# A joint-attention block on one Trainium2 core: the first key block's scale as a TensorE column, a copy put into VectorE's wait for the norm, and transposes spread over the waits for scale rows

## The chip, the cores and the metric

The kernel runs on one NeuronCore of a Trainium2 chip. The metric is the device time of one execution in microseconds, as the median over several runs; lower is better. A core has TensorE (matmuls and transposes, results into PSUM), VectorE, ScalarE and GpSimd (elementwise work), SyncE (here: it issues the loads), and DMA engines that move data between HBM and the core's SBUF. The engines run side by side, each through its own queue in order, and wait for one another by semaphores.

## The reference

One image stream (batch B = 2, 256 tokens) and one text stream (2 x 32 tokens), width D = 1152, all bf16. A conditioning vector `c` gives shift, scale and gate per stream; both streams attend jointly.

```python
mod_i = (_silu(c) @ wmod_img).reshape(B, 6, 1, D)       # the same for text
shi, sci, gai = mod_i[:, 0], mod_i[:, 1], mod_i[:, 2]
hi = _layernorm(x_img) * (1 + sci) + shi                 # the same for text
qkvi = hi @ wqkv_img
q, k, v = text and image tokens of each, concatenated
p = _softmax(einsum('bqd,bkd->bqk', q, k) * D ** -0.5)
a = einsum('bqk,bkd->bqd', p, v)
out_i = x_img + gai * (ai @ wo_img)
out_t = x_txt + gat * (at @ wo_txt)
```

## The kernel before

The width is cut into KT = 9 blocks of 128, the image tokens into four tiles of 128 (tiles 0 and 1 are batch 0, tiles 2 and 3 batch 1). Matmuls contract over the width, so activations must stand transposed: width on the partitions, tokens along the free dimension. "Key block kt" below is one block of 128 of that contracted width.

The work starts with v of the image. The shift is left out of it at first and added later (`shift_v_rows`), so v needs only the normed tokens times the scale 1 + `sci`. What happens before the first v matmul is the part that the change touches:

- *Loads.* SyncE issues all of them in one order: the two batches of `x_img` (L104), the scale weights `w_sc_i` in four pieces (L108: rows 0 to 3, 4 to 6, 7, 8; a row is 128 x 1152, 288 KB), the v weights `w_v_i` in six pieces (L110: rows 0, 1, 2, 3 to 4, 5 to 6, 7 to 8), then the other 1152 x 1152 matrices, each into one of five slots when the slot comes free.
- *silu(c)* stands as columns `sT` (128 x 9 x 2) and, padded with zeros to 32 columns, as `sT32`.
- *Norm.* Tiles 0 and 2 get their sums on ScalarE (`ln_sums`), tiles 1 and 3 their statistics on VectorE (`ln_stats`); ScalarE makes 1/std (`ln_rstd`), VectorE applies it (`ln_norm`, L212), into `xn_i`.
- *Transposes.* `x_transposes(k0, b)` (L240) transposes three key blocks of one batch on TensorE into a PSUM tile `tp` (six transposes of 128 x 128) and returns the function that copies them out to `xT_i` (L250): VectorE for k0 = 3, ScalarE for k0 = 0 and 6.
- *Scale rows.* `sc_rows` (L230) makes the scale as rows: for each kt, four matmuls of 288 columns side by side, each in a column tile of 32 of the array, into `sc_ps`; the first four add the 1. `sc_cols` (L256) turns blocks of it by VectorE's 32 x 32 transpose, so that the scale stands as a column per key block in `sc1_i`.
- *Scaling.* `x_scale` (L260) multiplies `xT_i` by that column into `hS_i`, on VectorE.
- *v.* `v_open` (L271) runs matmuls of 512 columns over several (token tile, column chunk) pairs; `A0` are the four pairs of batch 0, `A1` two of batch 1. The first call takes kt = 0, 1, 2 for `A0`, the next the same for `A1`.
- *Warm-ups.* `warm_up(n)` (L132) runs n matmuls of ones into `wps`, whose result nobody uses.

`pin` keeps each engine's instructions in the order in which the program has them; lines 292 to 328 are that order, written out by hand. PSUM has two pools: `ps_mm` with six buffers and `ps_tr` with two, given out in turn.

After v the program runs shift and second scaling, q and k of image and text, the scores, softmax, the attention over v, and the two output projections with the gates. TensorE works through them in program order.

Of the kernel before, what the change touches and what calls it, by code (L numbers as in the profile page):

```python
# [14 lines left out]
def kernel(  # L15
# [14 lines left out]
    nc = tc.nc  # L30
    bf = mybir.dt.bfloat16
    f32 = mybir.dt.float32
    PSUM = bass.MemoryType.PSUM

    B, NI, D = x_img.shape
    NT = x_txt.shape[1]
    P = 128
    KT = D // P
    NTOK = NI + NT
    NIT = (B * NI) // P  # L40
    TPB = NI // P
# [13 lines left out]
    ps_mm = ctx.enter_context(tc.tile_pool(name="ps_mm", bufs=6, space=PSUM))  # L55
    ps_tr = ctx.enter_context(tc.tile_pool(name="ps_tr", bufs=2, space=PSUM))

    pin = tc.keep_in_program_order

    def mm(*a, **k):  # L60
        return pin(nc.tensor.matmul(*a, **k))  # L61

    def tr(*a, **k):
        return pin(nc.tensor.transpose(*a, **k))  # L64
# [11 lines left out]
    def wtile(slot):  # L76
        return wpool.tile([P, KT, D], bf, tag="w%d" % slot, name="t")
# [4 lines left out]
    K8 = KT - 1  # L82
# [17 lines left out]
    w_sc_i = wtile(0)  # L100
# [21 lines left out]
    warm = const.tile([P, 512], bf)  # L122
# [3 lines left out]
    unit = const.tile([P, LW], bf)  # L126
# [5 lines left out]
    def warm_up(n):  # L132
        for _ in range(n):
            mm(wps[:], lhsT=warm[:, 0:P], rhs=warm[:], start=True, stop=True)
# [33 lines left out]
    sT = const.tile([P, KT, B], bf)  # L168
# [16 lines left out]
    def ln_stats(x_ap, np_, between=None):  # L185
        stats = small.tile([P, NCH, 6], f32, tag="stats")
        for k in range(NCH):
            if k == 1 and between:
                between()
            pin(nc.vector.bn_stats(stats[0:np_, k, :], x_ap[:, k * CH:(k + 1) * CH]))  # L190
        mv = small.tile([P, 2], f32, tag="mv")
        pin(nc.vector.bn_aggr(mv[0:np_, :], stats[0:np_, :, :]))
        return mv

    def ln_sums(x_ap, junk):
        sm = small.tile([P, 3], f32, tag="lnact")
        pin(nc.scalar.activation(junk, x_ap, ACT.Copy, scale=1.0 / D, accum_out=sm[:, 0:1]))
        pin(nc.scalar.activation(junk, x_ap, ACT.Square, scale=float(D) ** -0.5, accum_out=sm[:, 1:2]))
        return sm

    def ln_var(sm):
        pin(nc.vector.scalar_tensor_tensor(sm[:, 2:3], sm[:, 0:1], sm[:, 0:1], sm[:, 1:2],
                                           op0=ALU.mult, op1=ALU.subtract))

    def ln_rstd(var, np_, sign=1.0):
        rstd = small.tile([P, 1], f32, tag="rstd")
        pin(nc.scalar.activation(rstd[0:np_, :], var, ACT.Ln, bias=eps_t[0:np_], scale=sign))
        pin(nc.scalar.activation(rstd[0:np_, :], rstd[0:np_, :], ACT.Exp, scale=-0.5))
        return rstd

    def ln_norm(x_ap, mean, rstd, np_, out_ap):
        pin(nc.vector.tensor_scalar(out_ap, x_ap, mean, rstd[0:np_, :], op0=ALU.subtract, op1=ALU.mult))  # L212

    xn_i = act.tile([P, NIT, D], bf, tag="A")
    hS_i = act.tile([P, KT, B * NI], bf, tag="Bt")
    xT_i = act.tile([P, KT, B * NI], bf)
# [3 lines left out]
    def group(w, kt, g):  # L220
        return w[:, kt, :].rearrange("p (c g l) -> p g c l", g=NGG, l=LW)[:, g]

    def mod_cols_of(gps, name):
        t = const.tile([P, KT, LW], f32, name=name, tag={"sctc": "shc"}.get(name, name))
        pin(nc.vector.transpose(t[:].rearrange("p c l -> p (c l)"), gps[:].rearrange("p c l -> p (c l)")))
        return t

    sc_ps = ps_mm.tile([P, KT, LW], f32, tag="mm")

    def sc_rows(r0, r1):  # L230
        if r0 == 0:
            for g in range(NGG):
                mm(sc_ps[LW * g:LW * g + LW].rearrange("p c l -> p (c l)"), lhsT=unit[:], rhs=warm[:, 0:KT * LW],
                   start=True, stop=False, tile_position=(0, LW * g))
        for kt in range(r0, r1):
            for g in range(NGG):
                mm(sc_ps[LW * g:LW * g + LW], lhsT=sT32[:, kt, :], rhs=group(w_sc_i, kt, g),
                   start=False, stop=(kt == KT - 1), tile_position=(0, LW * g))

    def x_transposes(k0, b):  # L240
        tr_pool = b == 1 or k0 < 6
        tp = (ps_tr if tr_pool else ps_mm).tile([P, 3, NI], bf, tag="tr" if tr_pool else "mm", name="tp")
        for kt in range(k0, k0 + 3):
            for t in range(TPB):
                i = b * TPB + t
                tr(tp[:, kt - k0, t * P:(t + 1) * P], xn_i[:, i, kt * P:(kt + 1) * P], ident[:])
        dst = xT_i[:, k0:k0 + 3, b * NI:(b + 1) * NI]

        def copy_out():
            pin(nc.vector.tensor_copy(dst, tp[:]) if k0 == 3 else nc.scalar.copy(dst, tp[:]))  # L250

        return copy_out

    sc1_i = const.tile([P, KT, LW], f32, name="scc", tag="scc")

    def sc_cols(c0, c1):  # L256
        pin(nc.vector.transpose(sc1_i[:, c0:c1, :].rearrange("p c l -> p (c l)"),
                                sc_ps[:, c0:c1, :].rearrange("p c l -> p (c l)")))

    def x_scale(k0, k1, b, step=TPB):  # L260
        for kt in range(k0, k1):
            for t in range(0, TPB, step):
                t0, t1 = b * NI + t * P, b * NI + (t + step) * P
                pin(nc.vector.tensor_scalar(hS_i[:, kt, t0:t1], xT_i[:, kt, t0:t1], sc1_i[:, kt, b:b + 1], None,  # L264
                                            op0=ALU.mult))

    VW = 512
# [3 lines left out]
    def v_open(ids, k0, k1, kt_major=True):  # L271
        for key in ids:
            if key not in accs:
                accs[key] = ps_mm.tile([P, VW], f32, tag="mm", name="vps")
        loop = [(kt, key) for kt in range(k0, k1) for key in ids] if kt_major else \
            [(kt, key) for key in ids for kt in range(k0, k1)]
        for kt, (i, cc) in loop:
            mm(accs[(i, cc)][:], lhsT=hS_i[:, kt, i * P:(i + 1) * P], rhs=w_v_i[:, kt, cc * VW:(cc + 1) * VW],
               start=(kt == 0), stop=(kt == KT - 1), skip_group_check=True)
            if kt == KT - 1:  # L280
                evac(v_i[:, i, cc * VW:(cc + 1) * VW], accs[(i, cc)][:])
# [4 lines left out]
    def ln_norm_dve(i, mv):  # L286
        ln_norm(x_i[:, i, :], mv[:, 0:1], ln_rstd(mv[:, 1:2], P), P, xn_i[:, i, :])

    def ln_norm_act(i, sm):
        ln_norm(x_i[:, i, :], sm[:, 0:1], ln_rstd(sm[:, 2:3], P, sign=-1.0), P, xn_i[:, i, :])  # L290
# [3 lines left out]
    ln_var(s0)  # L294
    ln_norm_dve(1, m1)
    ln_norm_act(0, s0)
    s2 = ln_sums(x_i[:, 2, :], xn_i[:, 2, :])
    m3 = ln_stats(x_i[:, 3, :], P)
    ln_var(s2)
    r3, r2 = ln_rstd(m3[:, 1:2], P), ln_rstd(s2[:, 2:3], P, sign=-1.0)  # L300
    ln_norm(x_i[:, 3, :], m3[:, 0:1], r3, P, xn_i[:, 3, :])
    ln_norm(x_i[:, 2, :], s2[:, 0:1], r2, P, xn_i[:, 2, :])
    for out in [x_transposes(k0, 0) for k0 in (0, 3, 6)]:
        out()
    sc_rows(0, 4)
    warm_up(3)
    sc_rows(4, 7)
    out01 = x_transposes(0, 1)
    out31 = x_transposes(3, 1)
    sc_rows(7, K8)  # L310
    sc_rows(K8, KT)
    out61 = x_transposes(6, 1)
    out01()
    sc_cols(0, 1)
    x_scale(0, 1, 0, step=1)
    sc_cols(1, 5)
    x_scale(1, 3, 0)
    v_open(A0, 0, 3)
    out31()
    out61()  # L320
    x_scale(0, 3, 1)
    sc_cols(5, KT)
    for k0 in (3, 6):
# [436 lines left out]
```

## Time and profile before

| | us |
|---|---|
| median of 9 runs | 118.66 |
| lowest, highest | 118.17, 119.2 |
| the profiled execution | 119.2 |
| its span in the profile | 117.1 |
| TensorE busy (matmuls) | 111.0 |
| VectorE, ScalarE, GpSimd busy | 72.3, 44.2, 12.4 |
| first v matmul starts | 15.16 |

The profile is of one execution. PE is TensorE's matmuls, PEld its weight loads, DVE VectorE, ACT ScalarE, POOL GpSimd, SPq SyncE's queue of DMA issues. A line of a timeline has start, length, engine, source line, operation, what it writes and reads, the shape and the count of merged instructions, and in brackets the idle time before it with what ended it. The source line of a matmul is that of the helper `mm` (L61), of a transpose that of `tr` (L64), so those are told apart by what they write: `sc_ps` the scale rows, `tp` the transposes, `vps` v, `wps` the warm-ups. `t` stands for any weight matrix. The chain of waits follows the work that ended last back to its start: at each step to what released it, or to the instruction before it on its engine. A matmul's length in the trace includes the time in which it drains, so the pace of a row of them is read from start to start.

### The profile page before, as it was taken

The numbers are of one execution on the slowest core, as the hardware profiler recorded it, in microseconds if no ns is written. First come the engines' busy times: TensorE is split into PE (matmuls) and PEld (weight loads), VectorE is DVE, ScalarE is ACT, GpSimd is POOL, SyncE is SP. The second block draws the span as 40 slices with busy tenths as digits, with TensorE's granted clock in tenths as the row PEclk, the third lists the DMA queues.
The fourth block names the chain that finished last, engine by engine and source line by source line (L and its number), as shares of the span: only waits on it lengthen the run. The fifth ranks groups of instructions, "written<-read, shape, count | busy, mean of one in ns | idle before, by whom it ended". The sixth has DMA issues, their size and how long they took to land.

```text
span 117.1 us, 2569 instructions
## 1 busy us (share of the span) xinstructions
PE 111.0 (95%) x1072; PEld 63.6 (54%) x1072; DVE 72.3 (62%) x153; ACT 44.2 (38%) x92; POOL 12.4 (11%) x34
## 2 busy tenths in 40 slices
PE   5998799999999999999999999999999999999990
PEld 1245444444594444445444448787866666566670
DVE  3578296043787999999997040017758608666571
ACT  4799520023473288924330324135647500100000
POOL 7300000000000000000000000002450700451000
PEclk9999999999999999999999999999999999999999
DMA  3999999999999999999999999999999999822223
GB/s 109 368 342 395 404 411 405 412 412 410 412 405 406 314 392 411 407 409 412 413 351 403 411 412 413 405 411 405 412 405 409 408 423 366 318 103 58 101 50 101
DMA packets 18917, 41.02 MB, mean 350 GB/s; under 512 B 1323, under 2 KB 1851, under 8 KB 18907
## 3 DMA queue, kind: packets, MB, share of 16 engines
q1 hardware_dynamic: 18032, 39.85, 88.9%
q0 software_dynamic: 480, 0.89, 2.2%
q10 hardware_dynamic: 395, 0.12, 0.4%
q8 instruction: 8, 0.13, 0.4%
q14 instruction: 2, 0.02, 0.0%
HBM read 39.52 MB, written 1.34 MB: 349 GB/s over the span
## 4 chain that ended last, share of the span: by engine, by line
PE 84%; DMA 9%; DVE 2%; SPq 1%; ACT 1%; issue 1%; DVEq 0%
PE ps L61 52%; PE vps L61 15%; DMA t<-in_wmod_img_dram 9%; PE gps L61 5%; PE aps L61 5%; PE sps L61 4%; DVE tmp L701 1%; PE sc_ps L61 1%; DVE o L702 1%; SPq L104 1%; PE tp L64 1%; ACT pT L621 1%; PE pT_ps L64 0%; SPq L108 0%; PE tpt L64 0%
## 5 line engine op out<-in xcount | busy, mean ns | idle before, releaser
L61 PE MATMUL ps<-xT_i,t 128*128 128x512 bf16 x162 | 35.7, 380 | 0.0
L61 PEld LDWEIGHTS <-t 128*128 128x128 bf16 x324 | 20.5, 98 | 19.0 <-issue 0.6
L435 DVE SCALAR_TENSOR_TENSOR acc_sh<-t,sTf,acc_sh 128x1152 f32<-128x1152 bf16 x16 | 21.4, 1404 | 0.0
L61 PE MATMUL ps<-t,aT 128*128 128x384 bf16 (+3 forms) x153 | 20.3, 308 | 0.0
L61 PE MATMUL vps<-t,hS_i 128*128 128x512 bf16 (+1 forms) x108 | 17.9, 326 | 0.1
L61 PEld LDWEIGHTS <-aT 128*128 128x128 bf16 (+1 forms) x153 | 13.0, 101 | 7.1 <-issue 0.8
L61 PEld LDWEIGHTS <-hS_i 128*128 128x128 bf16 x108 | 9.0, 98 | 8.8 <-DVE hS_i L264 0.4
L365 ACT CAST qkT<-ps 128x512 bf16<-128x512 f32 (+2 forms) x11 | 6.1, 551 | 15.0 <-PE ps L61 13.7
L701 DVE TENSOR_TENSOR tmp<-ps,gb 128x384 bf16<-128x384 f32 (+2 forms) x13 | 6.8, 524 | 7.9 <-PE ps L61 4.1
L587 POOL TENSOR_SCALAR pb<-e,rs 128x32 bf16<-128x32 f32 (+1 forms) x5 | 2.2, 445 | 77.1 <-DVE rs L584 77.1
L61 PE MATMUL wps<-warm 128*128 128x512 bf16 x25 | 8.1, 482 | 1.5 <-DVE unit L127 1.5
L363 ACT ACTIVATE qkT<-ps 128x512 bf16<-128x512 f32 (+2 forms) x11 | 6.1, 561 | 8.7 <-PE ps L61 7.0
L180 DVE CAST v_i<-vps 128x512 bf16<-128x512 f32 x5 | 3.5, 692 | 7.5 <-PE vps L61 7.5
L572 DVE TENSOR_REDUCE nmx<-sps 128x1 f32<-128x288 f32 x4 | 1.8, 458 | 9.6 <-PE sps L61 9.6
L61 PEld LDWEIGHTS <-sT 128*32 128x32 bf16 x180 | 4.7, 96 | 3.6 <-issue 3.0
L182 ACT CAST v_i<-vps 128x512 bf16<-128x512 f32 x4 | 2.3, 580 | 9.9 <-PE vps L61 9.9
L634 DVE TENSOR_SCALAR aT<-aps,svc 128x288 bf16<-128x288 f32 x9 | 4.3, 517 | 2.2 <-PE aps L61 2.2
L61 PEld LDWEIGHTS <-warm 128*128 128x128 bf16 x25 | 2.7, 117 | 5.2 <-issue 2.4
L61 PE MATMUL sps<-qkT 128*128 128x288 bf16 (+1 forms) x54 | 5.3, 287 | 0.0
L61 PE MATMUL ps<-hT_t,t 128*128 128x64 bf16 x162 | 5.2, 194 | 0.0
L61 PE MATMUL gps<-t,sT 128*32 128x288 bf16 x144 | 5.2, 287 | 0.0
L61 PE MATMUL aps<-pT,v_i 128*128 128x288 bf16 x36 | 5.1, 287 | 0.1
(111 smaller groups left out, 105.2 us busy)
## 6 DMA issues: line engine op xcount, KB each, us to landing
t<-in_wqkv_txt_dram SPq DMA_DIRECT2D x3, 2592.0 KB, 18.8
t<-in_wmod_img_dram SPq DMA_DIRECT2D x2, 2592.0 KB, 13.8
t<-in_wmod_txt_dram SPq DMA_DIRECT2D x2, 2592.0 KB, 17.9
t<-in_wqkv_img_dram SPq DMA_DIRECT2D x3, 864.0 KB, 13.7
t<-in_wqkv_img_dram SPq DMA_DIRECT2D x1, 2592.0 KB
t<-in_wo_img_dram SPq DMA_DIRECT2D x3, 864.0 KB, 9.5
t<-in_wqkv_img_dram SPq DMA_DIRECT2D x3, 576.0 KB, 10.4
t<-in_wmod_txt_dram SPq DMA_DIRECT2D x2, 864.0 KB, 13.0
```

What stands on the lines that cost most here:

```text
L61: return pin(nc.tensor.matmul(*a, **k))
L64: return pin(nc.tensor.transpose(*a, **k))
L104: nc.sync.dma_start(x_i[:, b * TPB:(b + 1) * TPB, :], x_img[b].rearrange("(p t) d -> p t d", t=TPB))
L180: nc.vector.tensor_copy(out_ap, in_ap)
L182: nc.scalar.copy(out_ap, in_ap)
L363: nc.scalar.mul(out_ap, in_ap, SCALE)
L365: nc.scalar.copy(out_ap, in_ap)
L435: pin(nc.vector.scalar_tensor_tensor(acc, w_sh_t[:, kt, :], col, acc, op0=ALU.mult, op1=ALU.add))
L572: pin(nc.vector.reduce_max(nmx[0:qn, :], sps[0:qn, :], axis=AX.X, negate=True))
L587: pin(nc.gpsimd.tensor_scalar(pb[0:qn, NI + 2 * NT:NI + 3 * NT], e[0:qn, NI:NTOK], rs[0:qn, :], 0.0, op0=ALU.mult, op1=ALU.add))
L634: nc.vector.tensor_scalar(dst, tiles[(b, dt)][:], bias, None, op0=ALU.add)
L701: nc.vector.tensor_mul(tmp[:, 0:n], ps[:, 0:n], gb[:, b, c0:c0 + n])
```

## The change

1. `sc_first` is new: key block 0's part of the scale is also made directly as a column, by matmuls with `w_sc_i[:, kt, 0:128]` as the weights and the two columns of silu(c) as the moving operand, into `sc0_ps` (128 x 2). A first matmul of ones adds the 1. Its pieces follow those of `sc_rows`, and for the last two rows go ahead of them; `sc_rows` still runs over everything.
2. The first `x_scale` takes its scalar from `sc0_ps` in PSUM. The transpose `sc_cols(0, 1)` ahead of it is gone, and `sc_cols(1, 5)` becomes `sc_cols(0, 5)`.
3. `x_transposes` is taken apart into `x_tiles`, `x_transposes` and `x_out`. Batch 0's copy of k0 = 3 goes ahead of the norms of tiles 3 and 2 on VectorE. Batch 1's transposes of tile 3 for k0 = 3 and 6 go ahead of the scale rows 4 to 6, the other twelve ahead of rows 7 and 8; its three copies follow those, with VectorE's ahead of the first scaling.
4. One of three warm-ups goes. The k0 = 6 tile of each batch and `sc0_ps` are taken from `ps_mm`, in an order of their own.

```diff
+    sc0_ps = ps_mm.tile([P, B], f32, tag="mm")
+    tp60 = ps_mm.tile([P, 3, NI], bf, tag="mm", name="tp")
+    tp61 = ps_mm.tile([P, 3, NI], bf, tag="mm", name="tp")
     sc_ps = ps_mm.tile([P, KT, LW], f32, tag="mm")
+
+    def sc_first(r0, r1):
+        if r0 == 0:
+            mm(sc0_ps[:], lhsT=warm[:, 0:P], rhs=unit[:, 0:B], start=True, stop=False)
+        for kt in range(r0, r1):
+            mm(sc0_ps[:], lhsT=w_sc_i[:, kt, 0:P], rhs=sT[:, kt, :], start=False, stop=(kt == KT - 1))
...
-    def x_transposes(k0, b):
-        tr_pool = b == 1 or k0 < 6
-        tp = (ps_tr if tr_pool else ps_mm).tile([P, 3, NI], bf, tag="tr" if tr_pool else "mm", name="tp")
+    def x_tiles(k0, b):
+        return (tp61 if b else tp60) if k0 == 6 else ps_tr.tile([P, 3, NI], bf, tag="tr", name="tp")
+
+    def x_transposes(tp, k0, b, ts=range(TPB)):
         for kt in range(k0, k0 + 3):
-            for t in range(TPB):
+            for t in ts:
                 i = b * TPB + t
                 tr(tp[:, kt - k0, t * P:(t + 1) * P], xn_i[:, i, kt * P:(kt + 1) * P], ident[:])
+
+    def x_out(tp, k0, b):
         dst = xT_i[:, k0:k0 + 3, b * NI:(b + 1) * NI]
-
-        def copy_out():
-            pin(nc.vector.tensor_copy(dst, tp[:]) if k0 == 3 else nc.scalar.copy(dst, tp[:]))
-
-        return copy_out
+        pin(nc.vector.tensor_copy(dst, tp[:]) if k0 == 3 else nc.scalar.copy(dst, tp[:]))
...
-    def x_scale(k0, k1, b, step=TPB):
+    def x_scale(k0, k1, b, step=TPB, first=False):
...
-                pin(nc.vector.tensor_scalar(hS_i[:, kt, t0:t1], xT_i[:, kt, t0:t1], sc1_i[:, kt, b:b + 1], None,
+                pin(nc.vector.tensor_scalar(hS_i[:, kt, t0:t1], xT_i[:, kt, t0:t1],
+                                            sc0_ps[:, b:b + 1] if first else sc1_i[:, kt, b:b + 1], None,
                                             op0=ALU.mult))
...
     ln_norm_act(0, s0)
+    tps = [(x_tiles(k0, 0), k0, 0) for k0 in (3, 0, 6)]
+    for tp in tps:
+        x_transposes(*tp)
     s2 = ln_sums(x_i[:, 2, :], xn_i[:, 2, :])
     m3 = ln_stats(x_i[:, 3, :], P)
     ln_var(s2)
+    x_out(*tps[0])
     r3, r2 = ln_rstd(m3[:, 1:2], P), ln_rstd(s2[:, 2:3], P, sign=-1.0)
     ln_norm(x_i[:, 3, :], m3[:, 0:1], r3, P, xn_i[:, 3, :])
     ln_norm(x_i[:, 2, :], s2[:, 0:1], r2, P, xn_i[:, 2, :])
-    for out in [x_transposes(k0, 0) for k0 in (0, 3, 6)]:
-        out()
+    x_out(*tps[1])
+    x_out(*tps[2])
     sc_rows(0, 4)
-    warm_up(3)
+    sc_first(0, 4)
+    warm_up(2)
+    t3, t0, t6 = [(x_tiles(k0, 1), k0, 1) for k0 in (3, 0, 6)]
+    x_transposes(*t3, ts=(1,))
+    x_transposes(*t6, ts=(1,))
     sc_rows(4, 7)
-    out01 = x_transposes(0, 1)
-    out31 = x_transposes(3, 1)
-    sc_rows(7, K8)
-    sc_rows(K8, KT)
-    out61 = x_transposes(6, 1)
-    out01()
-    sc_cols(0, 1)
-    x_scale(0, 1, 0, step=1)
-    sc_cols(1, 5)
+    sc_first(4, 7)
+    x_transposes(*t3, ts=(0,))
+    x_transposes(*t6, ts=(0,))
+    x_transposes(*t0)
+    x_out(*t3)
+    x_out(*t6)
+    x_out(*t0)
+    sc_first(7, K8)
+    sc_first(K8, KT)
+    sc_rows(7, KT)
+    x_scale(0, 1, 0, step=1, first=True)
+    sc_cols(0, 5)
     x_scale(1, 3, 0)
     v_open(A0, 0, 3)
-    out31()
-    out61()
     x_scale(0, 3, 1)
```

## The prediction

> **What bounds the kernel now.** I read the page first, then the chain of waits in order of time, then the timeline around the one place where that chain is not TensorE's, and last the landings of the loads. On the page TensorE is busy almost all the time, and of the chain it holds 84%, a load 9% and VectorE 2%:
>
> ```profile
> PE 111.0 (95%) x1072; PEld 63.6 (54%) x1072; DVE 72.3 (62%) x153; ACT 44.2 (38%) x92; POOL 12.4 (11%) x34
> ...
> PE 84%; DMA 9%; DVE 2%; SPq 1%; ACT 1%; issue 1%; DVEq 0%
> ```
>
> The chain in order of time (start, length, what) shows where those 9% and 2% lie: all before 15.16 us, apart from the last two microseconds.
>
> ```profile
> 2.12 10.54 DMA t<-in_wmod_img_dram
> 12.66 0.04 issue
> 12.70 0.55 PE sc_ps L61 x12
> 13.26 0.78 PE tp L64 x12
> 14.03 0.47 PE sc_ps L61 x8
> 14.50 0.02 issue
> 14.53 0.23 DVE scc L257
> ...
> 14.85 0.26 DVE hS_i L264
> 15.11 0.05 issue
> 15.16 13.77 PE vps L61 x63
> 28.93 1.22 PE gps L61 x36
> ```
>
> From 15.16 us, the first matmul of v (`v_open`), TensorE runs on: 63 matmuls in 13.77 us are 0.219 each, and the chain stays with it until 112.5 us but for 0.7 us around one ScalarE copy at 86. So the kernel's time is the start of `v_open` plus a fixed rest of 101.9 us. The question is only when `v_open` can start.
>
> What stands before it is a race of loads. The scale weights come in four pieces; the trace has matmuls waiting for rows 4 to 6 until 12.66, and the four matmuls of the last row start at 14.17. The timeline of TensorE and VectorE from there:
>
> ```profile
> 14.17 0.31 PE L61 MATMUL sc_ps<-t,sT 128*32 128x288 bf16 x4
> ...
> 14.53 0.22 DVE L257 STREAM_TRANSPOSE scc<-sc_ps 128x32 f32<-128x32 f32 x1 [2.14 <-PE sc_ps L61]
> 14.58 0.49 PE L64 MATMUL tp<-ident,xn_i 128*128 128x128 bf16 x6
> 14.85 0.42 DVE L264 TENSOR_SCALAR hS_i<-xT_i,scc 128x128 bf16<-128x128 bf16 x2
> ```
>
> From last row to first v matmul: 15.16 - 14.17 = 0.99 us. But v needs its own weights too. The DMA view of the window of each issue gives row 0 of the v weights, issued at 4.04, 10.8 us to landing:
>
> ```profile
> t<-in_wqkv_img_dram SPq DMA_DIRECT2D x1, 288.0 KB, 10.8
> ```
>
> That is 14.84. Row 2, issued at 5.12, takes 11.2 (16.32), rows 3 and 4, issued at 5.94, take 11.8 (17.74). The row 0 load is 0.3 us ahead of its use today; it is the next thing that is late.
>
> **Part by part.**
>
> *Scale column.* Nine matmuls of two columns and one of ones are added (`sc_first`), with full 128x128 weights. Not in the trace; nearest row: the text matmuls of 64 columns with new weights each (`ps<-hT_t,t`), 43 in 1.43 us, 0.033 each. Upper bound: nothing overlaps, one weight load each, 0.098. I take 0.033. Five of the ten stand ahead of the warm-ups, in the wait for rows 4 to 6, and cost nothing there (without cover 0.17; one warm-up of 0.22 goes).
>
> *TensorE from 12.70.* Rows 4 to 6: 12.70 to 13.19, where today's transposes start. Three of `sc_first`: 0.10, to 13.29. Then 12 transposes as today (six have moved ahead of 12.66, six come from behind the scale rows): 0.77 less the 0.09 of the following switch of tile form, 0.68, to 13.97. Two of `sc_first` (rows 7, 8): row 7 is there by 13.96, as it didn't stop today's matmul; row 8 lets go at 14.17, as now. With the upper price the engine is there at 14.17 too (13.48 + 0.68), a tie that costs up to 0.1. End of a short matmul: 0.19 (the 64-column row), and 0.05 to VectorE: 14.41.
>
> *First scaling.* The VectorE transpose of 0.22 with its two hand-overs (14.53 to 14.85, 0.32) leaves the path. The scaling itself takes 14.85 to 15.16 today, 0.31 with the hand-over, and gives weights for `v_open` at 14.72. Its scalar now comes from PSUM; no row has that. By the rows that read PSUM (a 128x32 transpose 0.22, 128x768 copy 0.55) against those that don't (0.25, 0.58), PSUM costs nothing visible; a gain is excluded, as the work is the same. Upper bound 0.1: 14.82. Either is ahead of 14.84.
>
> *The rest of the scale rows.* `sc_rows(7, KT)`, eight matmuls, now stands between `sc_first` and v. [...] The trace shows the price: the last group of row matmuls starts at 12.95, the transposes behind it at 13.19, 0.24 where a group takes 0.12 (288 columns at the pace of 512 in 0.216), so about 0.1 per change. Sum: 14.20, two groups of 0.12, two changes: 14.64, under the cover of the scaling until 14.72 and of the load until 14.84. [...]
>
> *Start of v.* Row 0 lands at 14.84, and 0.04 for release (12.66 to 12.70): **14.88** against 15.16, **0.28 earlier**. That is all: the path through the scale could give 15.16 - 14.72 = 0.44, the load takes 0.16 of it back.
>
> *What VectorE must do next.* Five blocks of the scale are transposed at once from about 14.83 (the four-block row is 0.31, so 0.35): 15.18; key block 1 with hand-over by 15.50, and v needs it at 14.88 + 4 x 0.216 = 15.74. Covered by 0.24. The 0.55 copy that stood at 15.92 is gone from here.
>
> *Copies.* Batch 0's block copy (0.55) goes into VectorE's wait of 0.25 at 10.60, so the two norms end 0.30 later: 11.73 and 12.23. Behind them wait the batch-1 transposes: six of tile 3 at about 11.9 (six times 0.056, ending near 12.25, ahead of 12.66) and the others from 13.29. Covered by 0.4 and 1.1. Batch 1's three copies: VectorE's waits for three transposes from 13.29 (0.17, end 0.22, hand-over 0.05), 13.73 to 14.28, 0.13 ahead of the first scaling that is queued behind it; what it is later than that is paid beyond the 0.12 that row 0 covers. ScalarE's two, 0.80 each, run from 13.9 to 15.5, and the scaling of batch 1 asks for them at 15.7. The PSUM buffers shift by three places; all that `v_open` reuses are read out by 14.8.
>
> *Queues.* No DMA is issued or moved, so SyncE's and GpSimd's queues stay.
>
> *Later loads, asked for 0.28 sooner.* Row 2 of v: 16.36 against 14.88 + 8 x 0.216 = 16.61. Rows 3, 4: 17.74 against 18.77. The next 2.6 MB load (13.45 + 13.8 = 27.25) against 28.6. The tightest late one, 62.32 + 18.8 = 81.1, against 83.3. None stops it.
>
> **Sum.** Profiled execution: 119.2 us, span 117.1 (15.16 + 101.94), 2.1 around it; it becomes 118.9, span 116.8. It is the slowest of the nine runs; the median is 118.66, and since start and row landing shift together I take the same 0.28 off: **118.38 us** (-0.24%).
>
> **Rivals.**
> - *More (16%): 118.2.* The 0.16 of row 0 isn't there in the timed runs. Then the scale path decides: 0.44, 118.22. For it: the landing comes from one execution, the slowest. Against: the rows stand in one queue.
> - *Nothing (5%): 118.66.* A later row takes the gain back. Row 1 has no landing in the trace; its matmuls started at 16.03 today, so it may be as late as that. Against: rows 0 and 2 land at 14.84 and 16.32, and equal rows put it at 15.58, before 15.74.
> - *Slower (11%): 120.1.* [...]
> - *First case (68%): 118.38*, its own range 118.15 to 118.6.
>
> **Chances.** About 0.3% (0.36 us) is what a measurement here can tell from no change, and 0.28 lies just inside. Of the first case I give 26 of its 68 to a time measured beyond it, 42 within. Faster: 0.26 + 0.16 = 0.42. Same: 0.42 + 0.05 = 0.47. Slower 0.11. The range 118.05 to 118.8 takes in the first three cases with the unknown costs (up to 0.1 each) and leaves out the slower one.
>
> **What would show it.** In the profile after: the first `vps` matmul at about 14.88, released by the v weights' landing and not by `hS_i`; the first scaling at 14.4 with no transpose ahead of it; norms ending near 12.2; 63 `vps` matmuls again in 13.8. I am wrong if the first `vps` matmul still waits for VectorE, if matmuls stand 0.43 apart after 15 us, if a pause appears inside the `vps` run (row 1), or if v starts on time and a later load stops it.

## The result, and the profile after

The changed kernel takes 118.21 us (median of 17 runs, 117.44 to 118.63), the kernel before 118.69 in the same set (54 runs). The ratio is 0.9958, 95% interval 0.9937 to 0.9978: 0.42% faster, or 0.50 us, with 0.26 to 0.75 in the interval. Two later sets of the same kernel gave 0.9977 (0.9961 to 0.9993) and 0.9969 (0.9952 to 0.9985). 118.21 lies in the range; the direction is the one that the prediction gave 42 in 100, and in the traces 0.2 us of the gain came from a place that it had not looked at.

The page after, engines and chain:

```profile
PE 110.7 (96%) x1081; PEld 63.6 (55%) x1081; DVE 72.1 (62%) x152; ACT 44.2 (38%) x92; POOL 12.4 (11%) x34
...
PE 83%; DMA 9%; SPq 3%; DVE 2%; ACT 1%; issue 0%
```

The chain of waits after, in order of time:

```profile
4.01 10.12 DMA t<-in_wqkv_img_dram
14.13 0.04 issue
14.17 13.76 PE vps L61 x63
27.93 1.22 PE gps L61 x36
...
67.28 8.61 PE ps L61 x180
75.89 5.13 PE sps L61 x54
```

The load on the chain is now `wqkv`, the v weights, no longer `wmod`, the scale weights, and it hands over straight to v: no scale row, no VectorE line stands between. TensorE's timeline shows the new order:

```profile
11.73 0.51 PE L64 MATMUL tp<-ident,xn_i 128*128 128x128 bf16 x6 [0.39 <-DVE xn_i L212]
12.17 0.55 PE L61 MATMUL sc_ps<-t,sT 128*32 128x288 bf16 x12
12.66 0.23 PE L61 MATMUL sc_ps<-sT,t 128*128 128x2 bf16 x3
12.75 0.83 PE L64 MATMUL tp<-ident,xn_i 128*128 128x128 bf16 x12
13.41 0.26 PE L61 MATMUL sc_ps<-sT,t 128*128 128x2 bf16 x2
13.61 0.43 PE L61 MATMUL sc_ps<-t,sT 128*32 128x288 bf16 x8
14.17 3.83 PE L61 MATMUL vps<-t,hS_i 128*128 128x512 bf16 x17
```

And VectorE's, where the first scaling reads `sc_ps` (this is `sc0_ps`, buffer names are merged) with no transpose before it:

```profile
10.64 0.55 DVE L260 COPY xT_i<-tp 128x768 bf16<-128x768 bf16 x1
11.11 0.57 DVE L212 TENSOR_SCALAR xn_i<-x_i,mv,rstd 128x1152 bf16<-128x1152 bf16 x1
11.59 0.57 DVE L212 TENSOR_SCALAR xn_i<-x_i,sm,rstd 128x1152 bf16<-128x1152 bf16 x1
13.11 0.56 DVE L260 COPY xT_i<-tp 128x768 bf16<-128x768 bf16 x1 [0.95 <-PE tp L64]
13.79 0.43 DVE L272 TENSOR_SCALAR hS_i<-xT_i,sc_ps 128x128 bf16<-128x128 bf16 x2
```

In this execution the last scale row landed at 13.45 and v row 0 at 14.13. In the profile of before they landed at 14.13 and 14.83. So the spans, 115.9 and 117.1, must not be compared as they stand: 0.68 us of the 1.2 is only when the loads came. What belongs to the change is what follows the landing: the last row to the first v matmul took 1.03 us before (15.16 - 14.13), 0.72 after (14.17 - 13.45), **0.31 less**. And from the first v matmul to the end: 101.93 before, 101.70 after, **0.23 less**. The second part I had taken as fixed. It sits in one spot of the chain of before, which the prediction did not show:

```profile
68.28 7.36 PE ps L61 x137
75.63 0.04 issue
75.67 1.43 PE ps L61 x43
77.10 5.13 PE sps L61 x54
```

Before, from 68.28 to the scores at 77.10 TensorE needs 8.82 us for 180 matmuls; after it needs 8.61. In between, at 75.44 to 75.67, the text matmuls, otherwise 0.029 us apart, stop once for 0.21 us. No semaphore ends that pause; the "issue" line is all the chain has of it.

### The profile page after: what moved, and what is told of

It reads as the page before. It is cut to its first block, busy times and chain, and to the rows that moved or that the text cites. A ratio compares the mean times of both kernels' runs of the same rounds, so it can differ in the third digit from the quotient of the medians.

```text
span 115.9 us, 2586 instructions
## 1 busy us (share of the span) xinstructions
PE 110.7 (96%) x1081; PEld 63.6 (55%) x1081; DVE 72.1 (62%) x152; ACT 44.2 (38%) x92; POOL 12.4 (11%) x34
## 4 chain that ended last, share of the span: by engine, by line
PE 83%; DMA 9%; SPq 3%; DVE 2%; ACT 1%; issue 0%
PE ps L61 52%; PE vps L61 15%; DMA t<-in_wqkv_img_dram 9%; PE gps L61 5%; PE aps L61 5%; PE sps L61 4%; SPq L108 2%; DVE tmp L719 1%; DVE o L720 1%; SPq L104 1%; ACT pT L639 1%; PE pT_ps L64 0%; PE tpt L64 0%; PE shps L61 0%
```

## The experiments

Two questions: does the start of v set the gain, and by which of the change's parts; and what is the pause near 75 us? My theory was that v's start behind the last scale row gives 0.28 to 0.31 us and the pause another 0.2. The rivals: the reordering gains by itself; the pause is chance; the norms, or v's matmuls slower for the warm-up that goes, have a part in it.

What the traces show, in us from the span's start. A landing is the last of the sixteen parts of a load, read from the counts of its semaphore. "Gap" is from the landing of the last scale row to the first v matmul, "rest" from there to the end of the span, "pause" the one near 75 us.

| kernel | last scale row | v row 0 | v starts | gap | rest | pause |
|---|---|---|---|---|---|---|
| before | 14.13 | 14.83 | 15.16 | 1.03 | 101.93 | 0.21 |
| before again (e8) | 13.04 | 13.76 | 14.07 | 1.03 | 102.19 | 0.22 |
| after | 13.45 | 14.13 | 14.17 | 0.72 | 101.70 | none |
| after again (e5) | 13.24 | 13.97 | 14.01 | 0.77 | 102.26 | none |
| after, third (e12) | 13.17 | 13.86 | 13.90 | 0.73 | 101.70 | none |
| e1 scale column alone | 13.00 | 13.71 | 13.90 | 0.91 | 101.70 | none |
| e2 order alone | 13.12 | 13.83 | 14.16 | 1.04 | 101.92 | 0.21 |
| e3 late transposes | 13.28 | 13.99 | 14.04 | 0.76 | 101.85 | none |
| e4 before, padded | 13.37 | 14.06 | 14.40 | 1.03 | 101.71 | none |
| e6 copy back | 13.07 | 13.76 | 13.95 | 0.88 | 101.71 | none |
| e7 no warm-ups | 12.49 | 13.21 | 13.70 | 1.21 | 101.71 | none |
| e9 shifted by 256 | 13.84 | 14.54 | 14.58 | 0.74 | 101.77 | 0.07 |
| e10 lead | 13.50 | 14.22 | 14.26 | 0.76 | 101.70 | none |
| e11 lead, split loads | 13.35 | 13.69 | 13.93 | 0.58 | 102.13 | none |

**e1, the scale column alone** (all transposes and copies where they were):

```diff
     sc_rows(0, 4)
-    warm_up(3)
+    sc_first(0, 4)
+    warm_up(2)
     sc_rows(4, 7)
+    sc_first(4, 7)
...
-    sc_rows(7, K8)
-    sc_rows(K8, KT)
+    sc_first(7, K8)
+    sc_first(K8, KT)
+    sc_rows(7, KT)
...
-    sc_cols(0, 1)
-    x_scale(0, 1, 0, step=1)
-    sc_cols(1, 5)
+    x_scale(0, 1, 0, step=1, first=True)
+    sc_cols(0, 5)
```

> Part 1 and 2 alone: the scale column and the first scaling out of PSUM, one warm-up less, all transposes and copies in the places of the kernel before (six transposes of batch 1 stand between the scale rows and v). If the time comes from the start of v: from last scale row to first v matmul about 0.85 us (0.99 before, 0.72 after), as the six transposes (0.33) now end behind the scaling; time 0.15 us below before. If the reordering is what gains: no change.

Measured: ratio 0.9965 (0.9949 to 0.9981), 0.41 us below before, more than the 0.15 forecast for the start alone. The timeline of TensorE has the six transposes between the rows and v, as expected:

```profile
13.57 0.50 PE L64 MATMUL tp<-ident,xn_i 128*128 128x128 bf16 x6
13.90 2.32 PE L61 MATMUL vps<-t,hS_i 128*128 128x512 bf16 x9
```

The gap, 0.91, is 0.12 below before; the pause is gone as well (0.21). Together 0.33, inside the interval of the measured time (0.22 to 0.60).

**e2, the order alone** (the changed kernel without `sc_first`, with `sc_cols(0, 1)` ahead of the first scaling and three warm-ups).

> Part 3 alone: copy and transposes in the order of the changed kernel, the scale column left out, so that the first scaling waits for the transposed scale rows as before. If the start of v sets the time: the six transposes that leave the stretch were hidden beside VectorE's transpose and scaling, so last row to first v stays at 0.99 us and the time within 0.1 us of before. If the reordering gains by itself (VectorE's emptier queue behind the first scaling): 0.2 us or more below before.

Measured: 0.9998 (0.9979 to 1.0017). VectorE's transpose and scaling are the path again, TensorE idle beside them. VectorE, then TensorE:

```profile
13.52 0.22 DVE L258 STREAM_TRANSPOSE scc<-sc_ps 128x32 f32<-128x32 f32 x1 [0.32 <-PE sc_ps L61]
```

```profile
14.16 2.12 PE L61 MATMUL vps<-t,hS_i 128*128 128x512 bf16 x9 [0.69 <-DVE hS_i L265]
```

Gap and rest are those of before (1.04 and 101.92), so the reordering gains nothing by itself. That rival is out. With the column beside it the order does count: the gap is 0.91 in e1 and 0.72 to 0.77 in the changed kernel, where no transposes stand between the scale rows and v.

**e3, late transposes** (`x_transposes(*t3)` and `(*t6)` whole, behind `sc_first(4, 7)`).

> The changed kernel with the six transposes of token tile 3 put back behind scale rows 4 to 6, so that 18 instead of 12 stand between those and the last two rows. If TensorE's own queue decides once the transposes are there: six times 0.056 = 0.33 us more from rows 4 to 6 on, of which 0.04 (wait for the last row) and 0.07 (lead of the scaling over the v weights) are covered: v starts 0.2 us later than in the changed kernel, time 0.2 us above it. If the v weights' landing covers them: no difference to the changed kernel.

Measured: 0.9978 (0.9961 to 0.9996). The changed kernel has 0.9958, 0.9977 and 0.9969 in its three sets, and all these intervals overlap, so the times alone don't settle 0.2 us. The trace does: the gap is 0.76, as in the changed kernel, and v starts 0.05 behind row 0. My 0.2 us was a miss. TensorE:

```profile
11.68 0.55 PE L61 MATMUL sc_ps<-t,sT 128*32 128x288 bf16 x12 [0.76 <-DMA t<-in_wmod_img_dram]
...
12.25 1.17 PE L64 MATMUL tp<-ident,xn_i 128*128 128x128 bf16 x18
13.25 0.25 PE L61 MATMUL sc_ps<-sT,t 128*128 128x2 bf16 x2
```

All 18 transposes fit between rows 4 to 6 and the last row's landing at 13.28, since rows 4 to 6 start the moment they land. In the changed kernel the six early transposes wait for tile 3's norm and rows 4 to 6 stand behind them: there (timeline above) the rows landed at 11.97 and started at 12.17. What the early place saves is lost in front.

**e4, before with padding** (ten matmuls of two columns of ones for one warm-up; TensorE then has as many instructions as after).

```diff
-    warm_up(3)
+    for _ in range(10):
+        mm(wps[:, 0:B], lhsT=warm[:, 0:P], rhs=unit[:, 0:B], start=True, stop=True)
+    warm_up(2)
```

> The kernel before with ten idle two-column matmuls of ones for one of its three warm-ups, in the pause before scale rows 4 to 6, so that TensorE's program has the same number of instructions as the changed one; nothing else is changed. If only the start of v gains: no change to before. If the 0.21 us pause of TensorE at 75.4 us in the profile of before, which the changed kernel's profile lacks, depends on where the program's instructions fall in memory: no such pause in this profile and a time 0.2 us below before.

Measured: 0.9978 (0.9963 to 0.9992), 0.26 us (0.09 to 0.44) faster than before, with the gap still 1.03. The chain has no stop where before has one (the lines at 72.03 in this and 71.95 in e8 are one missing matmul record each). e4:

```profile
72.03 0.05 issue
72.08 4.04 PE ps L61 x88
76.12 5.13 PE sps L61 x54
```

**e8, before once more**, for its profile.

> The kernel before once more, for its profile. If the pause of 0.21 us at 75.4 us is steady: it is there again, in the same instruction of TensorE. If it is chance: it is missing or elsewhere.

Measured: one run, 118.35. The pause is there again, in the same place, with 43 matmuls to go:

```profile
71.95 0.05 issue
72.00 2.78 PE ps L61 x45
74.78 0.06 issue
74.84 1.43 PE ps L61 x43
```

So the pause is steady, and it goes with the number of TensorE instructions: it is in all three profiles with 1072 weight loads, one for each matmul (before, e2, e8), and in none of the ten with 1079 or 1081, whether `sc_first` or idle padding (e4) adds them. The trace also suggests a cause. A DMA queue of its own brings instructions (q8 on the page of before: 8 loads, 0.13 MB, so 16 KB each); I take them for TensorE's, which has 2144 of the page's 2569 instructions. In the DMA view of 73.3 to 74.4 us of before there is one such load:

```profile
q8 instruction: 1, 0.02, 5.3%
```

It starts at 73.36, takes 0.93 us, and the pause ends 2.31 us after its start. In e2 and e8 the load starts at 72.33 and 72.53, and the pause ends 2.34 and 2.31 later. In all ten kernels without the pause the same load starts at 66.3 to 67.2, ahead of the stretch of short matmuls, where TensorE takes one weight load and one matmul each 0.029 us. What starts the load late, and whether it alone stops TensorE, no run here isolates.

**e9, shifted by 256** (48 and 93 short warm-ups for 8 and 14 long ones).

> The changed kernel with its 8 and 14 warm-ups at the start cut into 48 and 93 shorter ones of about the same total time: 119 matmuls, and so with their weight loads 238 TensorE instructions, more. With the 18 more that the change brings that is 256 more than the kernel before, the distance of the instruction loads in the trace. If the pause near 75 us hangs on where the instruction loads fall: it is back (0.21 us), the start of v is as in the changed kernel, and the time 0.2 us above the changed kernel's of this call. If it was another effect of the change: no pause, same time as the changed kernel.

Measured: 1.0019 (1.0008 to 1.003), 0.59 us above the changed kernel of the same set. The 256 of its expectation is the distance of the first two instruction loads of before, not of all: 223, 479 and 685 matmuls and weight loads start ahead of the first three (16.97, 33.65 and 48.15 us), 256 and 206 apart. The load that comes before the pause is late again (72.57, as in before), and a pause is back, but of 0.07 us, ending 2.37 after the load's start. So the instruction count moves the load, as expected, but the pause came back at a third of its size: a late load and a pause go together in all four profiles that have either, while the length of the pause stays unexplained. And most of the loss is elsewhere. Rows 4 to 6 and v's weights are late:

```profile
12.49 0.55 PE L61 MATMUL sc_ps<-t,sT 128*32 128x288 bf16 x12 [0.50 <-DMA t<-in_wmod_img_dram]
...
14.58 1.67 PE L61 MATMUL vps<-t,hS_i 128*128 128x512 bf16 x6 [0.16 <-DMA t<-in_wqkv_img_dram]
```

The longer program has one more instruction load, at 9.73 us for 0.96 us, in the middle of the scale weights' transfer; no other kernel here has one before 15 us. The last part of rows 4 to 6 then lands 0.88 us behind the fifteenth, that of rows 0 to 3 before it only 0.48. That the load delays those weights fits, but wasn't tested apart.

**e5 and e12, the changed kernel again.**

> The changed kernel once more. If the start of v is all: 0.28 to 0.31 us below before, and the first v matmul 0.72 us behind the landing of the last scale row and 0.04 behind the landing of v row 0, whatever the loads do in this execution. If the missing pause at 75 us is a steady part: 0.5 us below before, and again no pause.

> The changed kernel on the same chip as the three before it, to compare with: 0.25 to 0.5 us below before, by how late the loads are on this chip (0.3 for the start of v where the last scale row lands after 13.3 us, less than 0.15 where it lands by 13.0, and 0.2 for the pause).

Measured: 0.9977 and 0.9969, 0.27 and 0.37 us, against 0.50 in the first set; neither has the pause. So e5's profile takes the second branch of its expectation (no pause), its time is nearer to the first (0.28 to 0.31), though its interval, 0.08 to 0.46, nearly reaches the second. e12's 0.37 lies in the range expected of it. v started 0.04 behind row 0 in all three profiles. But in e5 v ran into its own next load:

```profile
15.73 2.32 PE L61 MATMUL vps<-t,hS_i 128*128 128x512 bf16 x10
18.45 1.89 PE L61 MATMUL vps<-t,hS_i 128*128 128x512 bf16 x8 [0.40 <-DMA t<-in_wqkv_img_dram]
```

Rows 3 and 4 of v landed at 18.41, and the 0.56 us between the expected and the real start stay in the rest (102.26). e8, the kernel before, has the same wait with 0.24 us, e3 with 0.16, the other profiles none. An earlier v asks for these rows earlier; that it is caught more often for that is not shown.

**e6, copy back** (`x_out(*tps[0])` behind the two norms again).

> The changed kernel with batch 0's VectorE copy put back behind the two norms. If the norms are not on the path (as predicted): same time as the changed kernel. If the six early transposes gain from earlier norms: TensorE starts them 0.25 us sooner, ahead of rows 4 to 6 anyway, no gain in time. If the copy's old place delays the batch-1 copy or the first scaling: slower by up to 0.2 us.

Measured: 0.9989 (0.9974 to 1.0004), its interval overlapping e5's. The profile shows what the moved copy does, and I had not expected it:

```profile
11.65 0.49 PE L64 MATMUL tp<-ident,xn_i 128*128 128x128 bf16 x6 [0.75 <-ACT xT_i L260]
12.08 0.55 PE L61 MATMUL sc_ps<-t,sT 128*32 128x288 bf16 x12
```

The early transposes wait 0.75 us, not for tile 3's norm (done at 11.11) but for ScalarE's copy of batch 0, and rows 4 to 6, landed at 11.59, start at 12.08. With VectorE's copy late, the first PSUM buffer to come free for them is, as I read it, the one that ScalarE's copy empties. Only the early transposes need VectorE's early copy: e1, which has neither, gains as much in time.

**e7, no warm-ups** ahead of rows 4 to 6: do the matmuls of v then come further apart? In before the first eight matmuls, of 512 columns like those of v, take 3.59 us, 0.43 apart; v's come 0.219 apart (63 in 13.77).

> The changed kernel without the two warm-ups ahead of rows 4 to 6. [...]

Measured: 0.9968 (0.9951 to 0.9985). The rest after v's start is 101.71, 101.70 in the changed kernel, so the matmuls ran no slower, and the clock that the profile shows as granted is 1.00 throughout 10.5 to 17.1 us. The 22 runs lie between 117.40 and 118.09. The loads were the earliest of all here (last row 12.49), and v was at 13.70: TensorE had no idle time from the first early transpose at 11.39 to the last `sc_first` at 13.09. Where loads are that early, TensorE's own queue is the bound, with VectorE's copy of its transposes as the last link, queued ahead of the first scaling:

```profile
12.76 0.56 DVE L260 COPY xT_i<-tp 128x768 bf16<-128x768 bf16 x1 [0.94 <-PE tp L64]
13.38 0.43 DVE L272 TENSOR_SCALAR hS_i<-xT_i,sc_ps 128x128 bf16<-128x128 bf16 x2
```

The last `sc_first` had ended at 13.26, 0.06 ahead of that copy. e6 has the same order of ends (13.51 and 13.58).

**e10, lead**, and **e11, lead with split loads**, were tries at more. e10 has no warm-ups, the copy back, a PSUM buffer of its own for batch 1's k0 = 3 transposes, and a one-column VectorE copy that takes the wait for ScalarE early. e11 adds:

```diff
+    nc.sync.dma_start(w_v_i[:, 0:1, 0:512], v_v[:, 0:1, 0:512])
+    nc.sync.dma_start(w_v_i[:, 0:1, 512:D], v_v[:, 0:1, 512:D])
-    for r0, r1 in ((0, 1), (1, 2), (2, 3), (3, 5), (5, 7), (7, KT)):
+    for r0, r1 in ((1, 2), (2, 3), (3, 4), (4, 5), (5, 7), (7, KT)):
...
-    A0 = [(0, 0), (0, 1), (1, 0), (1, 1)]
+    A0 = [(0, 0), (1, 0), (0, 1), (1, 1)]
```

> Aimed at the path from the norms: the changed kernel without the two warm-ups, batch 0's copy behind the norms again, batch 1's k0 = 3 transposes in a PSUM buffer of their own so that they wait for no copy, and a one-column copy on VectorE that takes the wait for ScalarE's copy out of the first scaling. If TensorE's queue from the norm of tile 3 on bounds v where the loads are early: the first v matmul up to 0.3 us earlier than in the changed kernel there, 0.1 to 0.2 us less time. If the last scale row or v row 0 is always the bound: v at 0.72 us behind the last row, time within 0.05 us of the changed kernel.

> The kernel of the run before with v row 0 loaded in two pieces of columns (512 and 640), rows 3 and 4 loaded one by one, and the first four v matmuls of a key block in an order that asks for the first piece twice before the second. If v row 0 and rows 3 to 4 stop TensorE: v starts 0.57 us behind the last scale row where loads are late, no pause at the 18th v matmul, 0.1 us less than the run before. If two more loads on SyncE's queue delay the later ones: a pause inside the 63 v matmuls, slower.

Measured: e10 0.9959 (0.9945 to 0.9972), e11 0.9975 (0.9962 to 0.9988), the changed kernel beside them 0.9969 (0.9952 to 0.9985). e10 and the changed kernel have the same median, 117.77, and in e10's profile v starts 0.04 behind row 0 and 0.76 behind the last scale row: the second branch of its expectation. A gain of 0.1 us over the changed kernel is not shown. e11 confirms the bound and gains nothing from it: with half of row 0 landed at 13.69, v started 0.58 behind the last scale row, released by `hS_i` as forecast, yet its rest is 0.43 longer. Of that 0.07 is TensorE's (one short wait for `hS_i` in the v run), the remainder lies behind TensorE's last matmul. Why it lies there stays open.

## Why the prediction was right, and where it was not

The mechanism forecast for the start of v is the measured one. That the time came 0.17 us below the point given is not to its credit: the start accounts for 0.31 us, the rest is a pause that it had not seen, and the range was wide for other reasons.

- **What bounds it, and the start of v: right.** The prediction put v at 0.04 behind row 0's landing, 0.28 earlier. It is 0.04 behind row 0 in all three profiles of the changed kernel (in e5 the scaled tokens came at the same moment, and the trace names those), and 0.31 earlier counted from the last scale row.
- **The parts of that sum.** The short matmuls came 0.025 apart (0.033 taken) and ended after 0.18 (0.19). A scalar from PSUM cost nothing: two scalings 0.43 after, 0.42 before. At a change of tile form 0.11 lay between the starts (the last `sc_first` at 13.50, the rows at 13.61; 0.1 taken for the change), covered as the sum had it. One term was too small: the hand-over from TensorE to VectorE, 13.68 to 13.79, is 0.11 and not 0.05. This scaling waits for ScalarE's copy too, long done by then (12.75). The price of that second wait shows in e10 and e11, where the one-column copy takes it early: there the hand-over is 0.04, in the other profiles with `sc_first` 0.11 to 0.13. So weights for v were ready at 14.10, 0.03 ahead of row 0's 14.13, where the sum had 0.12. The rival "more", which gave the scale path 0.44, would have found about 0.38 (1.03 less the 0.65 from 13.45 to 14.10).
- **"A fixed rest of 101.9 us": wrong, by 0.2 us.** This is the step that failed. I read the chain as TensorE without a break and took the "issue" line at 75.63 for nothing. It was a pause of 0.21 us that hangs on how many instructions TensorE has had; the change brings 18 more and lost it, by no design, and that is luck. e4 has the padding alone and is 0.26 us faster. That a late instruction load makes the pause is likely and not shown. With 0.31 the sum is 0.52 of the 0.50 measured in the first set.
- **"Norms covered by 0.4 us": right only for a late load.** The cover was read from one execution, in which rows 4 to 6 landed at 12.66. In the nine profiles with the early transposes they landed at 11.1 to 12.5, and in seven of those the transposes, which wait for the norm or for a copy, held them up, by 0.2 us in the profile after. So the early place of these six gains nothing that e3 can show, nor does the early copy that they need. What counts is that no transposes stand behind the last scale row any longer (gap 0.91 in e1, 0.76 in e3).
- **"None of the later loads stops it": wrong in one of three profiles** (e5, 0.56 us; margin reckoned 1.0).
- **"Slower": right to give it little.** No run shows the 1.7 us that its 120.1 adds to 118.38. Even without both warm-ups nothing slowed down: e7's rest is 101.71, and its slowest run of 22 took 118.09. In e7's profile the early loads left TensorE busy for 2.13 of the 2.20 us from 10.5 to 12.7; what a longer idle stretch there would do is not shown.

Left open: in the later two sets the gain, 0.27 and 0.37 us, is below 0.52. Early loads with TensorE's queue as the bound, and late rows 3 and 4, both cut it in single profiles; how often each happens in the timed runs was not measured.

## What to carry to other kernels

When one engine carries the chain, ask what its start waits for next: here the scale path could give 0.38 us and the next load let through 0.31. Don't read covers and landings from a single execution; the last scale row landed anywhere from 12.49 to 14.13 us in these profiles. And before a gain of some tenths is put down to a change in the work, pad the old program to the same instruction count: here that alone was worth 0.21 us in the traces, against 0.31 for the start of v.

## What was not expected of the hardware

A load of 16 KB of instructions takes 0.88 to 0.97 us in the first load of these profiles; in the profiles where the fourth starts late (72.3 to 73.4 us), TensorE stands still for 0.21 to 0.22 us among matmuls of 64 columns that follow each other every 0.029 us. In e9, where the load at 72.57 is the fifth, it is 0.07. With a second wait on the first scaling the hand-over from TensorE was 0.11 us (after), without it 0.04 (e10, e11), 0.07 less, although what that wait was for had ended at 12.75 and the hand-over began at 13.68. And loads end raggedly: of the 16 parts of the load of v rows 3 and 4 in e5, fifteen had landed by 16.27 us and the last at 18.41. This also makes over half of the spread of the landings: the last part of the last scale row came 0.10 us behind the fifteenth in e7 (landing 12.49) and 1.00 in before (14.13). Why it lags is open.
